# Reading the moving columns of two matrix products by turns from two halves of each row

## The chip, the cores and the metric

The kernel runs on one core of one Trainium2 chip. The core has TensorE (called PE in the profile, with its weight loads as PEld), VectorE (DVE), ScalarE (ACT), GpSimd (POOL) and SyncE (SP, which issues the DMAs here). The metric is the device time of one execution in microseconds (us); lower is better.

## The reference

Three stages follow each other; everything is fp32.

```
q, k, v: (2, 12, 448, 64)
attn = softmax(mask(q @ k.T / 8)) @ v          # causal, per head
x    = attn, heads side by side                # (896, 768)
h    = x @ w_in                                # (896, 2048)
x    = (h * sigmoid(h)) @ w_out                # (896, 768)
h    = x @ w_in2                               # (896, 1024)
s    = h * softmax(h)
out  = ((s - mean(s)) / sqrt(var(s) + 1e-6) * g_ln) @ w_out2     # (896, 768)
```

## The kernel before, in words

All matrix products but those of the attention run on operands that are split in two fp32r parts, a high part (the value rounded to fp32r) and a low part (what is left of it); each block is then three matrix instructions, high times high, high weight times low activation, and low weight times high activation. They are named `wh`, `wl` for weights, `xh`, `xl` for the first input, `g_h`, `g_l` for the activations.

*Attention* (about the first 75 us). Twelve head pairs go through scores, maximum, exponential, normalization, transposes and the product with v. The order of all its instructions is written out by hand in the table `ORDER`. At its end each head pair lies in PSUM as 128 features x 448 tokens (`pvs[p]`); `pv_hi` (lines 252 to 258, on ACT eight times and on DVE four) rounds it into `xh`, and `pv_lo` (line 260) has DVE write what is left into `xl`. So x stands in SBUF with features over partitions and the 448 tokens of a batch in one row of a tile.

*First product* (`gemm1`, lines 366 to 373, from about 62 to 186 us). For each of 16 blocks of 128 hidden features and each of the two batches, six blocks of x are multiplied: the weight block stands still (128 columns) and 448 tokens of x are the moving columns. That is 16 x 2 x 6 x 3 = 576 matrix instructions. The first two hidden blocks of batch 0 are done inside the attention (steps `g` of `ORDER`). After each block `silu` (lines 375 to 381) works on its 448 tokens: ACT takes the sigmoid from PSUM, DVE multiplies it by h from PSUM, DVE rounds it into `g_h`, POOL writes the rest into `g_l`. PSUM has two pairs of banks for h, so that TensorE goes on with the next block meanwhile.

*Second product* (`mm2`, lines 495 to 500, from about 186 to 301 us). The same with 16 blocks of g and six output blocks: 6 x 2 x 16 x 3 = 576 matrix instructions of 448 moving columns. `evict2` splits its output into `yh`, `yl`.

*Third and fourth product* (from about 301 us on): `gemm3` (line 630) with weights as 512 moving columns, a chain of softmax and normalization, transposes of 128 columns (line 670), and `product` (line 689) with 384 moving columns.

*Weights* arrive by DMA in chunks of three blocks (`load_w`), are put together from two words by ACT and three DVE instructions (`conv_a` line 276, `sign_low` 281, `rest_high` 287, `shift_w` 297), rounded by ACT (`split_high`, line 303) and completed by POOL (`split_low`, line 307) into a ring of four chunks (`wring`). Each chunk serves 18 matrix instructions in the first two products. `feed` issues this work ahead of its use; nothing but the ring's four places holds it back.

Tiles are placed with small pads, so that the rows that move and the weights that stand still begin at fixed places modulo 256 bytes in each of the products.

Of the kernel before, what the change touches and what calls it, by code (L numbers as in the profile page):

```python
# [8 lines left out]
F32 = mybir.dt.float32  # L9
F32R = mybir.dt.float32r  # L10
U32 = mybir.dt.uint32
AF = mybir.ActivationFunctionType
ALU = mybir.AluOpType
AX = mybir.AxisListType

B, H, S, D = 2, 12, 448, 64
# [64 lines left out]
def fused(ctx, tc, qk, vv, w1, w2, w3, w4, gl, out):  # L81
    nc = tc.nc
# [20 lines left out]
    xhl = act.tile([128, 2, KD, T], F32R, name="x", tag="a")  # L103
    xh, xl = xhl[:, 0], xhl[:, 1]
    g_h, g_l = [None, None], [None, None]

    with tc.manual_schedule():
        att = pool("att", 2)
# [133 lines left out]
        pvs = {}  # L242
# [8 lines left out]

        def pv_hi(p, eng):
            b, hp = divmod(p, NP)
            dst = xh[:, hp, b * S:b * S + S]
            if eng is nc.vector:
                eng.tensor_copy(dst, pvs[p][:, :S])
            else:
                eng.activation(dst, pvs[p][:, :S], AF.Copy)

        def pv_lo(p):  # L260
            b, hp = divmod(p, NP)
            sl = slice(b * S, b * S + S)
            nc.vector.tensor_tensor(xl[:, hp, sl], pvs[p][:, :S], xh[:, hp, sl].bitcast(F32), ALU.subtract)

        wraw, wx, wsp = {}, {}, {}
        streams = {1: w1, 2: w2, 3: w3, 4: w4}
# [46 lines left out]
        def wblock(n, m):  # L313
            h, l = wsp[n, m // NB]
            o = 128 * (m % NB)
            return h[:, o:o + 128], l[:, o:o + 128]
# [49 lines left out]
        def gemm1(f, half, b, turn=None):  # L366
            ps, turn = gps[f, b], half if turn is None else turn
            for k in range(NB * half, NB * half + NB):
                wh, wl = wblock(1, f * KD + k)
                rh, rl = xh[:, k, b * S:b * S + S], xl[:, k, b * S:b * S + S]  # L370
                nc.tensor.matmul(ps[:, :S], wh, rh, start=turn == 0 and k % NB == 0, stop=False)  # L371
                nc.tensor.matmul(ps[:, :S], wh, rl, start=False, stop=False)  # L372
                nc.tensor.matmul(ps[:, :S], wl, rh, start=False, stop=turn == 1 and k % NB == NB - 1)  # L373

        def silu(f, b):
            ps = gps.pop((f, b))
            sg = sgr.tile([128, S], F32, name="sg", tag="sg")
            nc.scalar.activation(sg, ps[:, :S], AF.Sigmoid)
            nc.vector.tensor_tensor(sg, ps[:, :S], sg, ALU.mult)
            nc.vector.tensor_copy(g_h[b][:, f], sg)  # L380
            nc.gpsimd.tensor_tensor(g_l[b][:, f], sg, g_h[b][:, f].bitcast(F32), ALU.subtract)  # L381

# [28 lines left out]
        def g1drain(n):  # L411
            f, half = divmod(n, 2)
            if gm[0] is None:
                pss.release()
                gm[0] = pool("gm", 2, space=PS, side="right")
            turn = int((f, 0) in gps)
            if not turn:
                gps[f, 0] = gm[0].tile([128, 512], F32, name="ps", tag="gm")
            gemm1(f, half, 0, turn)
# [6 lines left out]
        def scores_ahead(p, n):  # L426
# [9 lines left out]
            "n": lambda p, n, u, e: norm(p, u, e), "T": lambda p, n, u, e: transp(p, u, n),  # L436
            "x": lambda p, n, u, e: evict(p, u, e), "P": lambda p, n, u, e: pv(p, n),
            "h": lambda p, n, u, e: pv_hi(p, e), "l": lambda p, n, u, e: pv_lo(p),
            "ca": lambda m, n, u, e: conv_a(1, m), "sh": lambda m, n, u, e: shift_w(1, m),
            "sl": lambda m, n, u, e: sign_low(1, m, xs), "rh": lambda m, n, u, e: rest_high(1, m),  # L440
# [4 lines left out]
        for step in ORDER.split():  # L445
            step, _, n = step.partition("/")
# [12 lines left out]
        g_l[0] = g0p.tile([128, KF, S], F32R, name="gl0", tag="gl")  # L459
        sgr = pool("sgr", 2, side="right")  # L460
        silu(0, 0)
        silu(1, 0)
        g1p = pool("g1")
        pad(g1p, 64)
# [4 lines left out]
        for f in range(KF):  # L469
            if f == 1:  # L470
                gps[f, 1] = gm.tile([128, 512], F32, name="ps", tag="gm")
            else:
                t = pair()
                for b in range(B):
                    if f >= 2 or b == 1:
                        gps[f, b] = t[b]
            for half in range(2):
                for b in range(B):
                    if f >= 2 or b == 1:
                        gemm1(f, half, b)  # L480
                m = 2 * f + half + 4
                feed_to(*((1, m) if m < N12 else (2, m - N12)))
            for b in range(B):
                if f >= 2 or b == 1:
                    silu(f, b)
# [8 lines left out]

        def mm2(ps, d, f, b):
            wh, wl = wblock(2, d * KF + f)
            rh, rl = g_h[b][:, f], g_l[b][:, f]
            nc.tensor.matmul(ps[:, :S], wh, rh, start=f == 0, stop=False)  # L498
            nc.tensor.matmul(ps[:, :S], wh, rl, start=False, stop=False)  # L499
            nc.tensor.matmul(ps[:, :S], wl, rh, start=False, stop=f == KF - 1)  # L500
# [10 lines left out]
        def block2(m, b):  # L511
            d, f = divmod(m, KF)
            if f == 0 and b == 0:
                if d < KD - 1:
                    yps[d, 0], yps[d, 1] = pair()
                else:
                    for z in range(B):
                        yps[d, z] = gm.tile([128, 512], F32, name="ps", tag="gm")
            mm2(yps[d, b], d, f, b)
            return d if f == KF - 1 else None  # L520
# [28 lines left out]
        for m in range(N3):  # L549
# [4 lines left out]
            sl = slice(CH * m, CH * m + CH)  # L554
# [369 lines left out]
```

## Time and profile before

| | us |
|---|---|
| median of 3 runs (427.58 to 428.25) | 427.58 |
| profiled execution: span, first to last instruction | 426.4 |
| PE busy | 417.8 (98%) |
| DVE busy | 347.4 (81%) |
| ACT busy | 237.4 (56%) |
| POOL busy | 202.8 (48%) |

The median is 1.2 us more than the span of the profiled execution; that much lies around the span. The profile takes a matrix instruction as busy from its start to a modelled end, and consecutive ones overlap; the pace of TensorE is therefore read from the distance between two starts, not from the duration of one.

### The profile page before, as it was taken

The page shows a single profiled execution, that of the slowest core. Times are in us where ns is not written, and L with a number is a line of the kernel's source. Part 1 is how long each engine was busy: PE and PEld are TensorE (multiplying, and loading weights), DVE is VectorE, ACT ScalarE, POOL GpSimd, SP SyncE. Part 2 cuts the span into 40 slices and gives each one's busy share as a digit, 9 for nine tenths or more (in the row PEclk, how much of TensorE's full clock was granted, in tenths as well). Part 3 has the DMA queues.
Part 4 walks back from the last instruction along what each step waited for, and adds up shares of the span by engine and source line. Part 5 has one row for each costly group of instructions (what it writes and reads, how often), then busy time and mean ns, then how long its engine had stood idle before and what let it go on. Part 6 is the DMA issues. An engine that isn't in the chain of part 4 may idle for free.

```text
span 426.4 us, 7442 instructions
## 1 busy us (share of the span) xinstructions
PE 417.8 (98%) x2593; PEld 371.7 (87%) x2593; DVE 347.4 (81%) x739; ACT 237.4 (56%) x551; POOL 202.8 (48%) x222
## 2 busy tenths in 40 slices
PE   8899999999999999999999999999999999899996
PEld 6677777899999999999999999999888888889996
DVE  3999999899999989879687878947977876448953
ACT  4999997444344444353433444435557666698420
POOL 2996954377776757573241424423300010198240
PEclk9999999999999999999999999999999999999999
DMA  8764502145243343436474757534033310011021
GB/s 252 248 260 147 164 11 74 38 148 150 81 144 108 115 118 104 117 108 187 142 225 125 226 147 235 164 106 148 2 111 84 103 37 2 9 49 55 20 75 56
DMA packets 19798, 50.03 MB, mean 117 GB/s; under 512 B 2352, under 2 KB 4528, under 8 KB 19760
## 3 DMA queue, kind: packets, MB, share of 16 engines
q1 hardware_dynamic: 19760, 49.56, 37.9%
q8 instruction: 20, 0.33, 0.3%
q14 instruction: 18, 0.15, 0.1%
HBM read 46.80 MB, written 2.75 MB: 116 GB/s over the span
## 4 chain that ended last, share of the span: by engine, by line
PE 82%; DVE 11%; ACT 5%; issue 1%; DVEq 0%; SPq 0%
PE h L372 8%; PE h L371 8%; PE h L373 8%; PE h L499 8%; PE h L498 8%; PE h L500 7%; PE x L249 4%; PE h L637 4%; PE h L639 4%; PE h L638 4%; PE x L159 3%; DVE e L189 3%; PE x L223 3%; PE x L169 2%; PE ps L499 2%; PE ps L498 2%
## 5 line engine op out<-in xcount | busy, mean ns | idle before, releaser
L307 POOL TENSOR_TENSOR wl<-wx,wh 128x384 fp32r<-128x384 f32 x64 | 77.1, 1207 | 87.1 <-ACT wh L303 83.5
L276 ACT ACTIVATE wr<-wr 128x384 f32<-128x384 f32 x96 | 52.7, 554 | 33.7 <-DMA wr<-w_in 33.5
L303 ACT ACTIVATE wh<-wx 128x384 fp32r<-128x384 f32 x64 | 33.3, 522 | 64.2 <-DVE wx L287 39.1
L287 DVE SCALAR_TENSOR_TENSOR wx<-wr,wx 128x384 uint32<-128x384 uint32 x96 | 66.6, 694 | 0.1
L372 PE MATMUL h<-x,wh 128*128 128x448 f32 x174 | 63.2, 363 | 0.0
L371 PE MATMUL h<-x,wh 128*128 128x448 f32 x174 | 63.1, 362 | 0.0
L373 PE MATMUL h<-x,wl 128*128 128x448 f32 x174 | 62.6, 360 | 0.0
L297 DVE TENSOR_SCALAR wr<-wr 128x384 uint32<-128x384 uint32 x96 | 59.5, 620 | 2.5 <-DMA wr<-w_in 2.1
L281 DVE SCALAR_TENSOR_TENSOR wx<-wr 128x384 uint32<-128x384 uint32 x96 | 58.9, 614 | 1.3 <-POOL gl L381 1.3
L499 PE MATMUL h<-gl,wh 128*128 128x448 f32 x160 | 58.1, 363 | 0.0
L498 PE MATMUL h<-gh,wh 128*128 128x448 f32 x160 | 58.0, 362 | 0.0
L500 PE MATMUL h<-gh,wl 128*128 128x448 f32 x160 | 57.6, 360 | 0.0
L209 POOL TENSOR_TENSOR e<-e,st 128x128 f32<-128x128 f32 (+3 forms) x70 | 44.0, 664 | 20.6 <-DVE st L202 15.6
L381 POOL TENSOR_TENSOR gl<-sg,gh 128x448 fp32r<-128x448 f32 x32 | 41.0, 1281 | 17.3 <-DVE gh L380 9.6
L195 ACT ACTIVATE e<-e,st 128x128 f32<-128x128 f32 (+3 forms) x84 | 43.6, 528 | 4.7 <-DVE st L189 4.7
L189 DVE CUSTOM_DVE_ANT_0 e<-x,mask 128x128 f32<-128x128 f32 (+3 forms) x84 | 32.9, 445 | 5.6 <-PE x L159 5.6
L371 PEld LDWEIGHTS h<-x,wh 128*128 128x128 f32 x174 | 32.7, 188 | 2.6
L373 PEld LDWEIGHTS h<-x,wl 128*128 128x128 f32 x174 | 32.5, 187 | 2.3
L372 PEld LDWEIGHTS h<-x,wh 128*128 128x128 f32 x174 | 32.7, 188 | 1.6
L637 PE MATMUL h<-w3h,y 128*128 128x512 f32 x84 | 33.2, 395 | 0.0
L639 PE MATMUL h<-w3h,y 128*128 128x512 f32 x84 | 32.9, 392 | 0.0
L638 PE MATMUL h<-w3l,y 128*128 128x512 f32 x84 | 32.6, 388 | 0.0
(204 smaller groups left out, 876.8 us busy)
## 6 DMA issues: line engine op xcount, KB each, us to landing
wr<-w_in SPq DMA_DIRECT2D x96, 384.0 KB, 3.6
qk<-qk_in SPq DMA_DIRECT2D x11, 480.0 KB, 5.1
v<-vv_in SPq DMA_DIRECT2D x12, 256.0 KB, 4.3
out<-o SPq DMA_DIRECT2D x12, 192.0 KB, 1.9
out<-o SPq DMA_DIRECT2D x4, 96.0 KB, 2.2
qk<-qk_in SPq DMA_DIRECT2D x2, 128.0 KB, 2.3
qk<-qk_in SPq DMA_DIRECT2D x1, 224.0 KB, 2.6
gain<-gl_in SPq DMA_DIRECT2D x1, 4.0 KB, 3.7
```

The lines of the kernel that those rows point to most:

```text
L276: nc.scalar.activation(high, high, AF.Copy, scale=DOWN)
L281: nc.vector.scalar_tensor_tensor(x.bitcast(U32), r[:, :, 1], 0x80000000, r[:, :, 0], ALU.bitwise_and, ALU.bitwise_or)
L287: nc.vector.scalar_tensor_tensor(xu, r[:, :, 1], 3, xu, ALU.logical_shift_left, ALU.bitwise_or)
L297: nc.vector.tensor_scalar(low, low, 29, None, ALU.logical_shift_right)
L307: eng.tensor_tensor(l, wx.pop((n, c)), h.bitcast(F32), ALU.subtract)
L371: nc.tensor.matmul(ps[:, :S], wh, rh, start=turn == 0 and k % NB == 0, stop=False)
L372: nc.tensor.matmul(ps[:, :S], wh, rl, start=False, stop=False)
L373: nc.tensor.matmul(ps[:, :S], wl, rh, start=False, stop=turn == 1 and k % NB == NB - 1)
L498: nc.tensor.matmul(ps[:, :S], wh, rh, start=f == 0, stop=False)
L499: nc.tensor.matmul(ps[:, :S], wh, rl, start=False, stop=False)
L500: nc.tensor.matmul(ps[:, :S], wl, rh, start=False, stop=f == KF - 1)
L637: nc.tensor.matmul(ps[:, n], yh[:, k, at], wh, start=k == 0, stop=False)
```

## The change

The tokens of a row are stored in another order: first the 224 even ones, then the 224 odd ones. The stores into `xh`, `xl` and the results of `silu` take every second column of PSUM at a time and write two runs of 224 columns. The matrix instructions of the first two products read their moving columns with a pattern of two dimensions, which takes one column from the first half, one from the second, and so on; the columns therefore enter TensorE in the order of the tokens, and PSUM holds them as before. The halves begin 224 x 4 = 896 bytes apart. No instruction is added, removed or moved: all engines have the same instructions in the same order and with the same sizes.

```diff
+    def woven(a):
+        return a.rearrange("p (z n) -> p n z", z=2)
+
+    def parted(a):
+        return a.rearrange("p (n z) -> p z n", z=2)
+
+    def two(a):
+        return a.rearrange("p (z n) -> p z n", z=2)
+
...
         def pv_hi(p, eng):
             b, hp = divmod(p, NP)
-            dst = xh[:, hp, b * S:b * S + S]
+            dst, src = two(xh[:, hp, b * S:b * S + S]), parted(pvs[p][:, :S])
             if eng is nc.vector:
-                eng.tensor_copy(dst, pvs[p][:, :S])
+                eng.tensor_copy(dst, src)
             else:
-                eng.activation(dst, pvs[p][:, :S], AF.Copy)
+                eng.activation(dst, src, AF.Copy)
...
-            nc.vector.tensor_tensor(xl[:, hp, sl], pvs[p][:, :S], xh[:, hp, sl].bitcast(F32), ALU.subtract)
+            nc.vector.tensor_tensor(two(xl[:, hp, sl]), parted(pvs[p][:, :S]), two(xh[:, hp, sl].bitcast(F32)), ALU.subtract)
...
-                rh, rl = xh[:, k, b * S:b * S + S], xl[:, k, b * S:b * S + S]
+                rh, rl = [woven(a[:, k, b * S:b * S + S]) for a in (xh, xl)]
...
             sg = sgr.tile([128, S], F32, name="sg", tag="sg")
-            nc.scalar.activation(sg, ps[:, :S], AF.Sigmoid)
-            nc.vector.tensor_tensor(sg, ps[:, :S], sg, ALU.mult)
+            h, s2 = parted(ps[:, :S]), two(sg)
+            nc.scalar.activation(s2, h, AF.Sigmoid)
+            nc.vector.tensor_tensor(s2, h, s2, ALU.mult)
...
-            rh, rl = g_h[b][:, f], g_l[b][:, f]
+            rh, rl = woven(g_h[b][:, f]), woven(g_l[b][:, f])
```

## Rows read from the trace of the kernel before

**Rows 1.** The page: busy time of TensorE; its granted clock in 40 slices.

```profile
PE 417.8 (98%) x2593; PEld 371.7 (87%) x2593; DVE 347.4 (81%) x739; ACT 237.4 (56%) x551; POOL 202.8 (48%) x222
...
PEclk9999999999999999999999999999999999999999
```

**Rows 2.** All waits of PE: waiter, releaser, us in total, times, longest.

```profile
PE tp L670 <- DVE area L675: 2.2, 3, 1.3
PE x L388 <- DVE x L383: 1.4, 1, 1.4
PE x L223 <- DVE st L189: 0.9, 1, 0.9
PE x L249 <- DVE aT L238: 0.2, 1, 0.2
```

**Rows 3.** Groups of PE: count | busy us, mean ns | idle before.

```profile
L371 PE MATMUL h<-x,wh 128*128 128x448 f32 x174 | 63.1, 362 | 0.0
...
L498 PE MATMUL h<-gh,wh 128*128 128x448 f32 x160 | 58.0, 362 | 0.0
...
L498 PE MATMUL ps<-gh,wh 128*128 128x448 f32 x32 | 11.6, 362 | 0.0
...
L371 PE MATMUL ps<-x,wh 128*128 128x448 f32 x18 | 6.9, 382 | 0.0
```

**Rows 4.** PE in time (start us, duration), 448 columns, 69 starts, first and last.

```profile
186.34 0.36 PE L498 MATMUL h<-gh,wh 128*128 128x448 f32 x1
...
199.94 0.36 PE L500 MATMUL h<-gh,wl 128*128 128x448 f32 x1
```

**Rows 5.** PE in time, 512 columns, 25 starts, then 384 columns, 25 starts.

```profile
353.94 0.39 PE L637 MATMUL h<-w3h,y 128*128 128x512 f32 x1
...
359.44 0.39 PE L637 MATMUL h<-w3h,y 128*128 128x512 f32 x1
...
361.52 0.34 PE L692 MATMUL ps<-b11h,d 128*128 128x384 f32 x1
...
365.69 0.33 PE L692 MATMUL ps<-b12h,d 128*128 128x384 f32 x1
```

**Rows 6.** PE in time: products of the warm-up; eight transposes of 128 columns.

```profile
1.93 0.95 PE L388 MATMUL x<-x 128*128 128x448 f32 x2
2.30 0.95 PE L388 MATMUL x<-x 128*128 128x448 f32 x2
2.67 0.95 PE L388 MATMUL x<-x 128*128 128x448 f32 x2
...
360.13 1.04 PE L670 MATMUL tp<-ident,e 128*128 128x128 f32 x8
```

**Rows 7.** One line: the transposes' duration (min/median/max).

```profile
L670 PE MATMUL tp<-ident,e x56: 272/272/329, 351.0 to 403.7; 128*128 128x128 f32 x56
```

**Rows 8.** Busy time by stretch: attention, then the first product.

```profile
20.00:60.00 40.00, 39.83 (x514) 28.47 (x512) 39.36 (x148) 39.85 (x132) 33.92 (x53) 1.00 0.49 164
80.00:140.00 60.00, 60.00 (x302) 56.25 (x301) 58.91 (x89) 25.56 (x53) 43.82 (x35) 1.00 0.39 117
```

**Rows 9.** Groups of DVE and ACT: reads of PSUM, contiguous, by shape.

```profile
L379 DVE TENSOR_TENSOR sg<-h,sg 128x448 f32<-128x448 f32 x29 | 18.0, 620 | 4.5 <-ACT sg L378 3.9
L263 DVE TENSOR_TENSOR x<-x,x 128x448 fp32r<-128x448 f32 x12 | 7.4, 613 | 0.5 <-ACT x L258 0.4
L507 DVE TENSOR_TENSOR y<-h,y 128x448 fp32r<-128x448 f32 x5 | 3.1, 625 | 13.7 <-ACT y L506 13.7
...
L256 DVE CAST x<-x 128x448 fp32r<-128x448 f32 x4 | 2.5, 620 | 0.0
...
L507 DVE TENSOR_TENSOR y<-h,y 128x64 fp32r<-128x64 f32 x5 | 1.1, 224 | 1.4 <-ACT y L506 1.4
...
L378 ACT ACTIVATE sg<-h 128x448 f32<-128x448 f32 x29 | 15.6, 537 | 10.6 <-DVE sg L379 6.1 <-POOL wl L307 4.5
...
L506 ACT ACTIVATE y<-h 128x448 fp32r<-128x448 f32 x5 | 2.7, 545 | 8.9 <-PE h L500 8.9
...
L506 ACT ACTIVATE y<-h 128x64 fp32r<-128x64 f32 x5 | 1.1, 223 | 3.5 <-DVE y L507 3.5
```

**Rows 10.** Groups of DVE from 80 to 140 us: chunks made ready.

```profile
L281 DVE SCALAR_TENSOR_TENSOR wx<-wr 128x384 uint32<-128x384 uint32 x18 | 9.8, 546 | 0.0
```

**Rows 11.** In time: POOL completes the fifth chunk, PEld first loads from it.

```profile
83.09 1.14 POOL L307 TENSOR_TENSOR wl<-wx,wh 128x384 fp32r<-128x384 f32 x1
...
85.74 0.19 PEld L373 LDWEIGHTS h<-x,wl 128*128 128x128 f32 x1
```

## The prediction

> **What bounds the kernel now.** I read the page's head first: TensorE is busy for 417.8 of 426.4 us, and its granted clock is full in all 40 slices, that is 2.4 GHz [rows 1]. The list of its waits comes second: together they are 4.7 us (2.2 + 1.4 + 0.9 + 0.2), none of them in the first or second product [rows 2]. So the time is the sum of what TensorE's instructions take one after the other, and what the change does to their pace counts in full. Third, how many there are: the six lines of the two products have 174 + 18 or 160 + 32 instructions each, 192 x 6 = 1152 [rows 3], where one line of each product stands, since the other two have the same counts. Fourth, their pace, from the starts in the timeline: 13.60 us over 68 distances, 0.2000 us for one of 448 columns [rows 4]. 1152 x 0.2000 = 230.4 us, more than half of the span, runs at this pace.
>
> What is in these 200.0 ns? At 2.4 GHz, one column per cycle, 448 columns take 186.7 ns. 13.3 ns are left over. For 512 columns the distance is 5.50 / 24 = 229.2 ns, 15.9 more than the columns' 213.3; for 384 it is 4.17 / 24 = 173.8 ns, 13.8 more than 160.0 [rows 5]. So the columns themselves already stream at about full pace and some 13 to 16 ns per instruction come on top, nearly the same for three sizes. The remainder is not there at half the pace: the warm-up's products of 448 columns start 0.373 us apart, which is 448 columns at 1.2 per ns with nothing left over, and a transpose of 128 columns takes (1.04 - 0.272) / 7 = 0.110 us, 106.7 at that pace and 3 left [rows 6, 7]. [...]
>
> **The change part by part.** No instruction comes, goes or moves; SP, POOL and all weight work are untouched. Two things differ.
>
> (a) The moving columns of 1152 matrix instructions come by turns from two places 896 bytes apart. No row of the trace shows such a read. Bounds from the nearest rows: at best nothing is left over, 186.7 ns, as in the warm-up; at worst the supply halves, since of each place only one column at a time is wanted, and 448 columns take the warm-up's 373 ns. That is 1152 x -13.3 ns = -15.4 us on one side and 1152 x +173.3 ns = +199.7 us on the other. Which? Each half is now read at 1.2 columns per ns, the pace at which the rows show nothing lost; if the two places can be read beside each other, part of the 13.3 ns goes. If each column is a fetch of its own, the pace halves. The trace's only reads at full pace are contiguous and give 200.0, nearest to the good end. I take half of what is left over as gone, 6.7 ns: 1152 x 6.7 = 7.7 us less.
>
> (b) ACT and DVE read PSUM in steps of two columns: `pv_hi` (8 on ACT, 4 on DVE), `pv_lo` (12 on DVE), and in `silu` 32 sigmoids on ACT and 32 products on DVE. Their writes are two contiguous runs of 224, which I cost at nothing. Now these read contiguously, and a DVE read of 448 columns takes 613 to 625 ns, one of 64 columns 224 ns: (625 - 224) / 384 = 1.04 ns per column [rows 9]. At best the step costs nothing; a gain is excluded, the same columns go through one at a time. On ACT it is (545 - 223) / 384 = 0.84 ns [rows 9]. At worst every column takes twice as long, 448 x 1.04 = +0.47 us on DVE and 448 x 0.84 = +0.38 us on ACT. I take nothing, which lies nearest to all rows at hand. In the first product TensorE's 60.00 of 60 us cover it; in the attention nothing does, since there DVE has 39.36 and ACT 39.85 of 40 us [rows 8].
>
> Does the faster TensorE wait for something else? In the first product a chunk of weights must be ready for each 18 instructions, now every 3.60 us, then every 18 x 193.3 = 3.48 us. DVE makes 18 chunks in 60 us, 3.33 each [rows 10], and the fifth chunk is complete at 84.23, 1.5 us before it is used [rows 11]. So the supply of weights holds, if narrowly.
>
> Sum: the profiled execution's span of 426.4 less 7.7 is 418.7; with the 1.2 us by which the median of the runs lies above that span it comes to **419.9 us**.
>
> **The rivals.**
>
> *One fetch for each column* (slower). Place: every matrix instruction of the two products. If SBUF hands TensorE a short contiguous piece per access, and neighbours in it serve the next columns, reading by turns throws the neighbours away. It decides from the point where the supply falls under 2.24 columns per ns (448 in 200.0). At half pace: 427.6 + 199.7 = 627 us. For it: what is left over at full pace says that the supply is near its edge. Against it: two places may keep a piece each. At a quarter of the pace (747 ns) it would be 427.6 + 1152 x 0.547 = 1057 us; of such a pace no row of TensorE gives a sign. [...]
>
> *The remainder belongs to the change of weights, not to the columns* (the edit does nothing). Each matrix instruction has its own weight load; if the 13.3 ns are the exchange of weights, they stay. For it: they hardly grow with the columns. Against it: the warm-up changes weights too and loses nothing. Time: 427.6 us.
>
> *Reads of PSUM in steps cost double* (slower, with TensorE's pace unchanged). Place: DVE. In the attention 16 such reads x 0.47 = 7.5 us in a stage where DVE is nearly always busy; I count half of it, 3.8 us, since TensorE shares that bound. In the first product one `silu` per chunk makes DVE's 3.33 us 3.80, less 0.06 us of idle time per chunk 3.74, against 3.60 of TensorE: 0.14 us short per chunk over 28 chunks is 3.9 us, and 1.5 us of lead go off it: 2.4 us. Together 427.6 + 6.2 = 434 us. It decides from about 0.3 us per read, where DVE's chunk is longer than TensorE's. [...]
>
> **How the numbers follow.** Chances: forecast 0.38 (412.2 with all that is left over gone, 426.7 with hardly any); nothing 0.16; PSUM reads 0.13 (428.5 to 437); one fetch for each column 0.33, of which 0.27 at about half pace (500 to 640) and 0.06 beyond. Faster than now by over 0.2% (0.9 us, about what a measurement of this kernel can tell from no change) is the forecast alone: 0.38; the same 0.16; slower 0.13 + 0.33 = 0.46. The cases have both signs: the forecast's own range is 412 to 426.7 us. The range for 8 in 10 has to take in the half pace, so it goes from 412 to 630; outside are about 0.02 below and, with part of the half pace that keeps something left over, 0.12 above.
>
> **What would show it.** The distance between two starts on lines 498 to 500 of before decides nearly all: 187 to 199 ns for the forecast, 200 for no effect, 373 or more for one fetch per column. Lines of the third product must still show 229 ns; if those change too, the cause is not the pattern. The durations of the sigmoid (now 0.537 us) and of DVE's product (0.620 us) show (b) [rows 9]; a wait of TensorE for POOL's or ACT's weights in the first product would show that the supply was short. If the distance is over 200 ns, the step that was wrong is the choice of the good end in (a).

## The result, and the profile after

The changed kernel takes 415.62 us (median; 415.41 to 416.96) against 427.77 us of the kernel before in the same comparison. The ratio is 0.9723 with a 95% interval of 0.9707 to 0.9739: 12.15 us or 2.8% faster. The span of its profiled execution is 413.7 us, 12.7 less than before. The time is inside the stated range and inside the forecast's own (412 to 426.7); the gain is larger than the 7.7 us that were forecast. The times of whole kernels, here and below, are medians of executions at the full granted clock (0.995 and more on average); a few others, among them the profiled one of the kernel with the first product alone, ran at 0.85 or less and are left out.

Line numbers of the changed kernel are 9 to 10 higher than before. First its page: busy time and granted clock, then the waits of TensorE.

```profile
PE 405.2 (98%) x2593; PEld 373.5 (90%) x2593; DVE 347.4 (84%) x739; ACT 237.3 (57%) x551; POOL 206.3 (50%) x222
...
PEclk9999999999999999999999999999999999999999
```

```profile
PE tp L680 <- DVE area L685: 2.0, 2, 1.3
PE x L398 <- DVE x L393: 1.4, 1, 1.4
PE x L232 <- DVE st L198: 0.9, 1, 0.9
PE x L258 <- DVE aT L247: 0.2, 1, 0.2
```

Clock and waits are those of [rows 1, 2]: 4.5 us of waits in place of 4.7, none of them in the first two products. Only the pace differs. The timeline of TensorE gives it: two starts of the second product that lie 78 distances apart, then two starts of the third that lie nine apart.

```profile
184.96 0.35 PE L508 MATMUL h<-gh,wh 128*128 128x448 f32 x1
...
199.72 0.35 PE L508 MATMUL h<-gh,wh 128*128 128x448 f32 x1
...
344.64 0.39 PE L647 MATMUL h<-w3h,y 128*128 128x512 f32 x1
...
346.70 0.39 PE L647 MATMUL h<-w3h,y 128*128 128x512 f32 x1
```

The second product now has 14.76 / 78 = 0.1892 us from start to start where [rows 4] gave 0.2000; the third, which was not changed, has 2.06 / 9 = 0.229 as in [rows 5]. 1152 x 10.8 ns = 12.4 us, which is about the whole difference (12.15 us between the medians, 12.7 between the spans). The engines that now read PSUM in steps take as long as before [rows 9]; the groups by line, columns as there:

```profile
L389 DVE TENSOR_TENSOR sg<-h,sg 128x448 f32<-128x448 f32 x29 | 17.9, 618 | 1.1
L272 DVE TENSOR_TENSOR x<-x,x 128x448 fp32r<-128x448 f32 x12 | 7.4, 613 | 0.4 <-ACT x L267 0.3
...
L388 ACT ACTIVATE sg<-h 128x448 f32<-128x448 f32 x29 | 15.5, 535 | 10.7 <-DVE sg L389 10.7
```

### The profile page after: what moved, and what is told of

The parts are those of the page before. It is cut to its first block, busy times and chain, and to the rows that moved or that the text cites. A ratio compares the mean times of both kernels' runs of the same rounds, so it can differ in the third digit from the quotient of the medians.

```text
span 413.7 us, 7456 instructions
## 1 busy us (share of the span) xinstructions
PE 405.2 (98%) x2593; PEld 373.5 (90%) x2593; DVE 347.4 (84%) x739; ACT 237.3 (57%) x551; POOL 206.3 (50%) x222
## 4 chain that ended last, share of the span: by engine, by line
PE 88%; DVE 7%; ACT 3%; issue 1%; DVEq 0%; SPq 0%
PE h L380 8%; PE h L382 8%; PE h L381 8%; PE h L509 7%; PE h L508 7%; PE h L510 7%; PE x L258 4%; PE h L649 4%; PE h L648 4%; PE h L647 4%; PE ps L704 4%; PE ps L703 4%; PE ps L702 4%; PE x L168 3%; PE x L232 3%; DVE e L198 3%
## 5 line engine op out<-in xcount | busy, mean ns | idle before, releaser
L316 POOL TENSOR_TENSOR wl<-wx,wh 128x384 fp32r<-128x384 f32 x64 | 81.4, 1274 | 72.8 <-ACT wh L312 50.5
L285 ACT ACTIVATE wr<-wr 128x384 f32<-128x384 f32 x96 | 54.4, 569 | 35.4 <-DMA wr<-w_in 35.1
L296 DVE SCALAR_TENSOR_TENSOR wx<-wr,wx 128x384 uint32<-128x384 uint32 x96 | 69.1, 720 | 0.1
L382 PE MATMUL h<-x,wl 128*128 128x448 f32 x174 | 61.3, 352 | 0.0
L380 PE MATMUL h<-x,wh 128*128 128x448 f32 x174 | 61.3, 352 | 0.0
L381 PE MATMUL h<-x,wh 128*128 128x448 f32 x174 | 61.3, 352 | 0.0
L306 DVE TENSOR_SCALAR wr<-wr 128x384 uint32<-128x384 uint32 x96 | 57.5, 599 | 4.3 <-DMA wr<-w_in 4.1
L509 PE MATMUL h<-gl,wh 128*128 128x448 f32 x160 | 56.4, 352 | 0.0
L508 PE MATMUL h<-gh,wh 128*128 128x448 f32 x160 | 56.4, 352 | 0.0
L672 POOL TENSOR_TENSOR s<-s,mhalf 128x1 f32<-128x1 f32 x7 | 3.8, 549 | 60.2 <-DVE s L671 60.2
L649 PE MATMUL h<-w3h,y 128*128 128x512 f32 x84 | 33.1, 394 | 0.0
```

Source lines behind the costliest of these rows:

```text
L285: nc.scalar.activation(high, high, AF.Copy, scale=DOWN)
L296: nc.vector.scalar_tensor_tensor(xu, r[:, :, 1], 3, xu, ALU.logical_shift_left, ALU.bitwise_or)
L306: nc.vector.tensor_scalar(low, low, 29, None, ALU.logical_shift_right)
L316: eng.tensor_tensor(l, wx.pop((n, c)), h.bitcast(F32), ALU.subtract)
L649: nc.tensor.matmul(ps[:, n], yl[:, k, at], wh, start=False, stop=k == KD - 1)
```

## The experiments

**One product at a time.** In the first kernel only `gemm1` reads by turns and only x is laid out in halves; in the second only `mm2` and the activations.

```diff
-            rh, rl = woven(g_h[b][:, f]), woven(g_l[b][:, f])
+            rh, rl = g_h[b][:, f], g_l[b][:, f]
...
-            h, s2 = parted(ps[:, :S]), two(sg)
+            h, s2 = ps[:, :S], sg
```

> Only the first product reads by turns; x is laid out in halves, the activations as before. Theory A (the gain is the pace of the matrix instructions that read by turns, 200.0 ns before and 189.2 ns after): 576 x 10.8 ns = 6.2 us less than before, 421.5 us; starts 189 ns apart in the first product, 200 in the second. Theory B (the gain comes from elsewhere, such as the shifted timing of weights and DMAs): no such split; one of the two halves would carry nearly all 12 us.

Measured: 421.27 us, ratio to before 0.9847 (0.9828 to 0.9865).

```diff
-                rh, rl = [woven(a[:, k, b * S:b * S + S]) for a in (xh, xl)]
+                rh, rl = xh[:, k, b * S:b * S + S], xl[:, k, b * S:b * S + S]
```

> Only the second product reads by turns; x is contiguous, silu lays its results out in halves. Theory A: 576 x 10.8 ns = 6.2 us less than before, 421.5 us; starts 200 ns apart in the first product, 189 in the second. Theory B: nearly all of the 12 us or nearly nothing, as the other half has it.

Measured: 421.33 us, ratio 0.9847 (0.9831 to 0.9863). The timeline of TensorE in this kernel has both paces, two starts of the first product 51 distances apart and two of the second 75 apart:

```profile
169.65 0.36 PE L381 MATMUL h<-x,wh 128*128 128x448 f32 x1
...
179.85 0.36 PE L381 MATMUL h<-x,wh 128*128 128x448 f32 x1
...
185.65 0.35 PE L508 MATMUL h<-gh,wh 128*128 128x448 f32 x1
...
199.84 0.35 PE L508 MATMUL h<-gh,wh 128*128 128x448 f32 x1
```

10.20 / 51 = 0.200 us, then 14.19 / 75 = 0.189. The gains are 6.4 us each against the runs of before in that comparison (427.7), where theory A had 6.2. Together they are 0.7 us more than the 12.15 of both, which is no more than the intervals leave open (some 0.8 us each): theory A holds, and theory B, by which one half would carry nearly all, falls. The pace inside the kernel with the first product alone was not read.

**The stores alone.** The layout in halves stays, the matrix instructions read contiguously (both diffs on `rh, rl` above); what would put the tokens back in order is left out of this kernel.

> Only the stores change: x and the activations are laid out in halves and PSUM is read in steps of two, while the matrix instructions read contiguously as before (so the tokens enter the products in another order, and the output is in another order too). Theory A: 427.8 us, as before, within 0.2%; starts 200 ns apart; ACT and DVE reads of PSUM as long as before (0.54 and 0.62 us). Rival (reads of PSUM in steps cost something that the faster products hide in the changed kernel): up to 434 us, and DVE's product over 0.7 us.

Measured: 427.8 us, ratio 0.9998 (0.9988 to 1.0008). The same groups as above, in this kernel:

```profile
L389 DVE TENSOR_TENSOR sg<-h,sg 128x448 f32<-128x448 f32 x29 | 18.0, 621 | 4.5 <-ACT sg L388 3.9
L272 DVE TENSOR_TENSOR x<-x,x 128x448 fp32r<-128x448 f32 x12 | 7.4, 614 | 0.5 <-ACT x L267 0.4
```

A step of two columns in PSUM costs DVE nothing that the rows show (0.621 and 0.614 us against 0.620 and 0.613), nor ACT (0.535 us in the changed kernel against 0.537), so the rival of the PSUM reads falls, and not because something hides it.

**What about the pattern?** A kernel of streams of 24 equal instructions, one line of code for each pattern, as in

```
for i in range(24):
    nc.tensor.matmul(ps, W[:, 0:128], X[:, 16:464].rearrange("p (z n) -> p n z", z=2), start=True, stop=True)
```

> Leaves the whole computation of the reference out: one core runs streams of 24 equal fp32r matrix instructions each, with 128 x 448 moving columns unless said, and only the pattern of the moving columns, their place modulo 256 bytes against the weights, their number, or the number of weight columns changes. Read from it: the distance of two starts. Theory C (the weight load of the next instruction and the moving read meet in the same part of SBUF, and the contiguous read at full pace has no slack to make up for it): contiguous 448 differs with its place, 198 to 215 ns; with 64 or 32 weight columns in place of 128 the surplus over 186.7 falls from about 13 ns to about 7 and 3; by turns about 189 ns at any place. Theory D (a contiguous read at full pace has a fixed start-up of 13 ns of its own, whatever the weights do): 200 ns at every place and with every number of weight columns. Of the pattern: if the distance of the two places matters (parts of SBUF that repeat every 256 bytes), 896 and 1152 bytes apart give 189 ns and 1024, 768 and 512 bytes give 200 or more; if only the change from place to place matters, all give 189. If pieces of 2, 4 or 8 columns by turns serve as well as single ones, it is not the single column that matters.

A row of the timeline is one whole stream; the start of the next one less its own start, by 24, is the distance of two starts. In order: contiguous 448 at 0, 32 and 64 bytes past the place of the weights, and the next stream; contiguous 256, and the next; contiguous 448 with 32 weight columns in place of 128, at 64 bytes, and the next; by turns from places 960, then 1024 bytes apart, and the next; 256 columns by turns from places 512 bytes apart, and the next; by turns in pieces of 2 and 4 columns, and the next; steps of two columns, of four, and the next. The granted clock is 1.00 in all of them.

```profile
22.96 5.12 PE L32 MATMUL ps<-X,W 128*128 128x448 f32 x24
27.92 5.07 PE L34 MATMUL ps<-X,W 128*128 128x448 f32 x24
32.82 4.97 PE L36 MATMUL ps<-X,W 128*128 128x448 f32 x24
37.63 5.09 PE L38 MATMUL ps<-X,W 128*128 128x448 f32 x24
...
74.40 3.04 PE L54 MATMUL ps<-X,W 128*128 128x256 f32 x24
77.27 4.33 PE L56 MATMUL ps<-X,W 128*128 128x384 f32 x24
...
91.78 5.12 PE L62 MATMUL ps<-X,W 128*32 128x448 f32 x24
96.74 5.03 PE L64 MATMUL ps<-X,W 128*64 128x448 f32 x24
...
119.76 4.70 PE L74 MATMUL ps<-X,W 128*128 128x448 f32 x24
124.30 4.70 PE L76 MATMUL ps<-X,W 128*128 128x448 f32 x24
128.84 4.70 PE L78 MATMUL ps<-X,W 128*128 128x448 f32 x24
...
154.16 2.90 PE L90 MATMUL ps<-X,W 128*128 128x256 f32 x24
156.90 4.07 PE L92 MATMUL ps<-X,W 128*128 128x384 f32 x24
...
173.84 7.08 PE L100 MATMUL ps<-X,W 128*128 128x448 f32 x24
180.75 5.29 PE L102 MATMUL ps<-X,W 128*128 128x448 f32 x24
185.87 5.22 PE L104 MATMUL ps<-X,W 128*128 128x448 f32 x24
...
201.70 9.69 PE L110 MATMUL ps<-X,W 128*128 128x448 f32 x24
211.21 9.88 PE L112 MATMUL ps<-X,W 128*128 128x448 f32 x24
220.90 9.72 PE L114 MATMUL ps<-X,W 128*128 128x448 f32 x24
```

Contiguous takes 207 ns at 0 bytes and 200 at 64. With a quarter of the weight columns it takes 207 at 64 bytes, so longer than with all of them, where theory C wanted 3 ns of surplus: the number of weight columns does not make the surplus. Two other signs of theory C did come, though: the contiguous pace differs with the place, and by turns it is 189 ns at each of the places tried. And the weights have some part in it: the same moving columns take 205 ns with the weights at one place and 200 with weights 160 bytes further on (lines 46 and 50 of this kernel, not shown). What makes up the 0 to 7 ns above 200 is thus open; the 11 ns from 200 to 189 are the question of the second kernel of streams, below. Theory D, which wanted 200 at every place, falls. By turns it is 189 ns at each of eight distances between 896 and 1280 bytes, 1024 among them, so parts of SBUF that repeat every 256 bytes are not it either. But by turns in pieces of two columns takes 288 ns and in pieces of four 213 (of 8 and 16 columns 211, not shown): only single columns serve. Steps of two columns take 396, of four 404.

**The whole kernel with pieces of two.**

```diff
     def woven(a):
-        return a.rearrange("p (z n) -> p n z", z=2)
+        return a.rearrange("p (z n u) -> p n z u", z=2, u=2)
 
     def parted(a):
-        return a.rearrange("p (n z) -> p z n", z=2)
+        return a.rearrange("p (n z u) -> p z n u", z=2, u=2)
 
     def two(a):
-        return a.rearrange("p (z n) -> p z n", z=2)
+        return a.rearrange("p (z n u) -> p z n u", z=2, u=2)
```

> The changed kernel with the turns taken two columns at a time: two from the first half, two from the second, with the layout and the steps in PSUM to match. If the pace in the probe (287 ns for 448 columns against 189 by single columns) holds in the kernel: 415.6 + 1152 x 0.098 = 528 us. [...]

Measured: 527.27 us, ratio 1.233 (1.2302 to 1.2359). Two starts of the first product, 42 distances apart:

```profile
219.91 0.46 PE L380 MATMUL h<-x,wh 128*128 128x448 f32 x1
...
231.95 0.46 PE L380 MATMUL h<-x,wh 128*128 128x448 f32 x1
```

12.04 / 42 = 0.287 us: what the streams show holds in the kernel. Two halves of a row that are taken two columns at a time in place of one turn 12 us of gain into 100 us of loss.

**Which step is it?** The second kernel of streams gives the addresses directly (step and count per dimension) and tries other types.

> Leaves the whole computation out, as the first pattern probe: streams of 24 equal matrix instructions, 448 moving columns, 128 weight columns, only the addresses of the moving columns or their type change. [...] Theory F (memory in parts that repeat: two columns taken together must lie in different parts): 189 for some of the distances between 8 and 256 bytes and 200 to 400 for others, in a regular way; steps of 4 within the halves stay at 189. [...]

Again one row per stream. In order: contiguous; by turns; by turns with the places 8 bytes apart, and the next; by turns with each half itself in steps of 2, 3 and 4 columns; by turns from eight places and from four, and the next; then bf16 contiguous, by turns, in steps of 2, 4 and 8 columns. The granted clock is 1.00 up to 224 us.

```profile
22.69 4.97 PE L45 MATMUL ps<-X,W 128*128 128x448 f32 x24
27.50 4.70 PE L47 MATMUL ps<-X,W 128*128 128x448 f32 x24
...
36.58 4.70 PE L51 MATMUL ps<-X,W 128*128 128x448 f32 x24
41.12 4.71 PE L53 MATMUL ps<-X,W 128*128 128x448 f32 x24
...
86.52 4.96 PE L73 MATMUL ps<-X,W 128*128 128x448 f32 x24
91.32 7.36 PE L75 MATMUL ps<-X,W 128*128 128x448 f32 x24
98.52 9.71 PE L77 MATMUL ps<-X,W 128*128 128x448 f32 x24
108.05 10.52 PE L79 MATMUL ps<-X,W 128*128 128x448 f32 x24
118.36 6.11 PE L81 MATMUL ps<-X,W 128*128 128x448 f32 x24
124.31 4.77 PE L83 MATMUL ps<-X,W 128*128 128x448 f32 x24
...
193.51 4.70 PE L93 MATMUL ps<-XB,WB 128*128 128x448 bf16 x24
198.05 10.34 PE L95 MATMUL ps<-XB,WB 128*128 128x448 bf16 x24
208.23 4.89 PE L97 MATMUL ps<-XB,WB 128*128 128x448 bf16 x24
212.96 9.68 PE L99 MATMUL ps<-XB,WB 128*128 128x448 bf16 x24
222.45 19.10 PE L101 MATMUL ps<-XB,WB 128*128 128x448 bf16 x24
```

Take the even and the odd columns of a read as two sequences of 224, and look at the step within one. By turns it is 4 bytes (one column): 189 ns. Contiguous, or by turns with each half in steps of two, it is 8 bytes: 200 both times. With 12 bytes it is 300, with 16 bytes 397. That is 25.0, 25.0 and 24.8 ns for each byte of the step: from 8 to 16 bytes the times rise in proportion to it, with next to nothing left that all three would have in common, such as a change of weights. 4 bytes would be 100 ns at this rate, less than the 186.7 of 448 columns at 2.40 per ns, the pace by turns (53.3 ns for 128 columns more, lines 92 and 94 of the first kernel). Steps of 32 bytes (404) and of 64 (378, a stream of the first kernel that is not shown) cost about what 16 do; what ends the rise was not shown. By this reading the contiguous read is held up by the 8 bytes by which each of the two sequences advances, and by turns each advances by only 4. That the even and the odd columns count each by themselves is worked out from these paces and not seen as such. Theory F falls, since every distance tried from 8 bytes on gives 189, and steps of four columns within the halves take 397 where it wanted 189. Nor do two sequences that lie close disturb each other: 8 bytes apart, or the same column twice, is also 189. That the pattern's form with two dimensions helps by itself is ruled out by the halves in steps of two, which have the same form and 200 ns.

Reads by which a sequence alternates between places are slow, 248 ns from four places and 430 from eight, as are pieces of two columns (288). The steps do not give these: the slowest of them took 404 ns, and 430 is even more. Why is left open.

**More of the kernel by turns.** The third product's weights are laid out with even and odd columns apart within each 512, and read by turns; then the same for the fourth product's within each 384.

```diff
-                    wh, wl = w3h[:, o:o + 512], w3l[:, o:o + 512]
+                    wh, wl = woven(w3h[:, o:o + 512]), woven(w3l[:, o:o + 512])
...
-        "w3": chunks(inputs["moe2_w_in"].reshape(KD, 128, 2, 512).transpose(1, 2, 0, 3)),
+        "w3": chunks(inputs["moe2_w_in"].reshape(KD, 128, 2, 256, 2).transpose(1, 2, 0, 4, 3)),
```

> The changed kernel, and the third product reads its 512 moving columns by turns too (the weights lie with even and odd columns apart within each 512). If the pattern alone makes the pace: 252 x (229.0 - 215.8) ns = 3.3 us less than the changed kernel, 412.3 us, unless the chains of softmax between its blocks of tokens, which start when a block is done, hold TensorE up instead. Rival (it served because x and the activations are written by ACT, DVE and POOL meanwhile, while these weights lie still by then): no gain, 415.6 us.

Measured: 413.18 us, ratio to before 0.9664 (0.9646 to 0.9681), 2.4 us below the changed kernel. The rival falls: weights that lie still gain as well. The gain is 0.9 us short of the 3.3 that were worked out. In the profiled execution the granted clock was 0.51 from 354.9 to 358.3 us, 0.9 us after a wait of the transposes for 1.7 us had ended, and matrix instructions of 384 columns started 0.32 us apart there in place of 0.173, some 1.5 us in all. An execution with a mean clock of 1.000 took 412.64 us, one with 0.999 413.67, so whether this is what is missing stays open.

```diff
+                rh, rl = woven(bh[:, k]), woven(bl[:, k])
-                nc.tensor.matmul(ps, ah[:, k], bh[:, k], start=first and k == 0, stop=False)
+                nc.tensor.matmul(ps, ah[:, k], rh, start=first and k == 0, stop=False)
...
-        "w4": chunks(inputs["moe2_w_out"].reshape(KF2, 128, 2, CH).transpose(1, 2, 0, 3)),
+        "w4": chunks(inputs["moe2_w_out"].reshape(KF2, 128, 2, CH // 2, 2).transpose(1, 2, 0, 4, 3)),
```

> As the kernel with three products by turns, and the fourth reads its 384 moving columns by turns as well, from two places 768 bytes apart. By the pattern probe 312 x (173.8 - 162.6) ns = 3.5 us less than the kernel with three, 408.8 us, if TensorE sets the pace there; less, if the evictions and stores at the end set it: then between 409 and 412 us. If TensorE waits for ACT's and DVE's operands in that stage already, hardly any gain: 412 us.

Measured: 411.59 us, ratio 0.9625 (0.9612 to 0.9638): faster than both kernels, but 1.6 us below the one with three where 3.5 were worked out. TensorE's waits at the transposes, first in the kernel with three, then in this one; the others are the same 2.5 us as before:

```profile
PE tp L680 <- DVE area L685: 1.7, 1, 1.7
...
PE tp L680 <- DVE s L664: 0.2, 1, 0.2
```

```profile
PE tp L680 <- DVE area L685: 4.3, 3, 1.7
...
PE tp L680 <- DVE s L664: 0.6, 1, 0.6
```

The transposes (line 680) wait 4.9 us for DVE where the kernel with three has 1.9 (1.7 + 0.2). Of these, 4.3 are for the split of earlier transposes (line 685), which in DVE's order stands between the steps of the chain of softmax and normalization, and 0.6 for a step of the chain itself (line 664). The 3.0 us more of waiting fit the 1.9 us that are missing: a faster fourth product reaches the transposes sooner, and about half of the saving is lost there. That this is the cause was not tested by a run.

## Why the prediction was right, and where not

- *TensorE's pace counts in full*: right. 1152 x 10.8 ns explain 12.4 of the 12.7 us between the two spans, and each product has its half (6.4 us each alone).
- *The good end or the bad one in (a)*: the choice was right, the reason given for it only in part. With 0.38 against 0.33, and no row of such a read, there was luck in it. I argued that two places read beside each other might give the columns at full pace. The two places are not needed, 8 bytes apart or the same column twice does as well. What counts, by the streams, is that each of the two sequences of columns advances by 4 bytes instead of 8 (189 ns, 200 ns).
- *Half of what is left over*: this is the term that was mis-sized. I took 6.7 of 13.3 ns for want of any row, measured were 10.8; 2.5 ns stay at 448 columns. On 1152 instructions that is the difference between 7.7 and 12.4 us.
- *Some 13 to 16 ns per instruction on top, nearly the same for three sizes*: a wrong reading of right numbers, as the streams have it. What the runs show of 2.4 GHz and one column per cycle is the pace, 2.40 columns per ns at a granted clock of 1.00 in the first kernel of streams: by turns 384 columns take 162.5 ns and 512 take 215.8, 53.3 ns for 128 more. The contiguous 200 ns for 448 columns are 2.24 per ns, which gives 171 ns for 384 columns and 229 for 512 and fits [rows 5] (173.8, 229.2) to within 3 ns: the columns were not at full pace, the step of 8 bytes set it. Sizes alone do not tell it from a fixed part: 256 contiguous columns take 119.6 ns, 13 more than their 106.7, just as I read it, where 2.24 per ns gives 114. What tells it are the steps (200, 300, 397 ns), and that the gain by turns grows with the size: 5.4 ns for 256 columns (7.9 with the places further apart), 11.3 for 384, 11.2 for 448, 13.4 for 512, where a fixed part would give the same for all. That 256 contiguous columns take some 5 ns more than this is left open. Nor need the transposes of [rows 6, 7] show half the pace: 128 fp32r columns take 109 to 110 ns too, contiguous and by turns, twice their 53 (first kernel of streams, not shown), so something else holds instructions this short.
- *PSUM in steps costs nothing*: right, by the kernel with the stores alone (0.9998).
- *The supply of weights holds*: right; no wait of TensorE in the first product at 189 ns, faster than the 193.3 that I worked with.
- *One fetch for each column* was given 0.33 and did not come: 189 ns in place of 373 or more. About half the pace is there in other reads: a step of two columns takes 396 ns, and pieces of two (288 ns) and bf16 by turns (424 ns) at least go the same way. What one access hands over was not shown by any run; the runs show that the cost rises up to steps of 16 bytes within a sequence (200, 300, 397 ns for 8, 12 and 16) and no further (404 for 32), and that by turns each sequence advances by 4.
- *The remainder belongs to the change of weights*: excluded for the 10.8 ns, which go while the weights stay as they are, and by times that follow the step alone (200, 300, 397 ns). For the 2.5 ns that stay, and for the up to 7 ns by place, it is not excluded.

## What to carry to other kernels

Where TensorE streams fp32r without waits, compare the distance of two starts with the columns at the granted clock (2.40 per ns at 1.00 here) before looking for other work to save: contiguous fp32r reads of 384 to 512 columns ran 7 to 11% above it here, and storing even and odd columns apart, at no cost in the engines that write them, took all but 2.5 ns of it away. The order must alternate column by column, and it is not for bf16, whose contiguous read already runs at 189 ns and by turns takes 424. Weights can be laid out like this too, as in the third and fourth product here, until another wait ends last.

## What the runs showed of the hardware that was not expected

- In bf16 the times rise with the step from each column to the next, for one sequence of all 448 columns: steps of 4, 8 and 16 bytes take 197, 395 and 788 ns ((19.10 - 0.97) / 23 for the last, with 0.97 us for its single instruction), that is 49 ns for each byte of the step. So the two sequences were seen for fp32r alone. By turns (424 ns) does not fit, since its columns lie some 448 bytes apart and steps of 16 already take 788. In the stream with steps of 16 bytes the granted clock fell from 1.00 to 0.50 at 224.4 us, after the third start, while TensorE ran on without a gap, and the starts stayed 0.79 us apart before and after: this pace did not follow the clock.
- For plain fp32, where an instruction has two records in the trace, the patterns differ as well: 376 ns per record contiguous, 393 in steps of two, 473 by turns.
- Contiguous fp32r reads took 200 to 207 ns with the place of the columns against the weights modulo 256 bytes, at a granted clock of 1.0: 207, 204, 200, 205 and 203 ns at 0, 32, 64, 96 and 128 bytes. The kernel before has a place with 200. Why is left open.
